# Inverses of the first two steps of a chunked recurrence: by doubling on TensorE instead of by elimination on VectorE

## The chip, the cores and the metric

One core of a Trainium2 chip. The metric is the device time of one execution in microseconds (us). Engines are named as in the profile: PE is TensorE (matmul), PEld its weight loads, DVE is VectorE, ACT is ScalarE, POOL is GpSimd, SP is SyncE, which here only issues DMAs. All data is fp32.

## What is computed

A recurrent attention block, and a feed-forward block on its output. For each of 4 batches and 8 heads, over 768 positions with head dimension 40:

```python
for t in range(S):
    y[:, :, t] = np.einsum('bhd,bhde->bhe', rt, state)
    Sa = np.einsum('bhde,bhe->bhd', state, at)
    state_decay = state * wt[:, :, None, :] - np.einsum('bhd,bhe->bhde', Sa, bt)
    state = state_decay + np.einsum('bhd,bhe->bhde', vt, kt)
```

Then, with the 8 x 40 head outputs of a token side by side as `x` (3072 tokens x 320):

```python
h = x @ w_in                          # 320 -> 1024
e = np.exp(h - h.max(-1, keepdims=True))
solu = h * e / (e.sum(-1, keepdims=True) + 1e-09)
ln = (solu - mean) / np.sqrt(var + 1e-06) * g_ln
out = ln @ w_out                      # 1024 -> 320
```

The weights arrive as 64-bit floats and are turned into fp32 on the chip from their bits.

## The kernel before, in words

The 768 positions are cut into 12 chunks of 64, the 4 batches into 2 pairs; that makes N = 24 steps, step `i` being chunk `i // 2` of pair `i % 2`. A step holds 16 units (2 batches x 8 heads), each with 64 x 64 matrices, so that a tile of 128 partitions x 512 holds all 16.

Within a chunk each position depends on the earlier ones through a strictly triangular 64 x 64 matrix per unit, `nt`; the kernel needs the inverse of (1 + `nt`), called `tu`. It comes about as follows:

- `decay` (ACT and PE: logarithm, running sum `pcum`, exponentials `ei` and `inv`), `decay_turned` (PE transposes `pei`, ACT copies to `ex`), `scaled` (POOL: keys `kb` from `raw_b` or `raw_k` and `inv`), `front` (PE transposes `pa`, `pb`; DVE makes `aT`, ACT `bT`), `norm` (PE products `pnt`; DVE masks them to `nt`, L340) prepare a step.
- `norm` also writes `nt` to DRAM (`nt_dram`). For each pair of steps (`GRP` = 2) `spread` reads it back so that each 32 x 32 diagonal block lies along a partition (`blk`), and `invert` eliminates column by column on DVE: 30 times a product (L392, `prod`) and a difference (L394, `uu`). It is a generator: `begin_inverse(n)` starts pair `n`, `some(k)` does `k` of its columns, so that the columns of a pair are strewn among other work by hand.
- The block inverses go to DRAM (`uu_dram`); `bring` loads them to `tu` and `uh`, `flip` (DVE, L419) transposes a block, and `couple` and `close` (PE `py`, `pz`; ACT `wy` and a copy) build the off-diagonal block, which completes `tu`.
- With it the main chain of a step runs: `attend_kv` and `attend_rs` (transposes `pk`, `pv`, `pr`, `pst`), `scores` (PE `ps`; DVE masks to `psi` and into `lv`), `carried` and `driven` (`px`), `solved` (`pu`), `answered` (`pl`; DVE masks to `lu`), `read` (`pyo`), `leave` (DVE, POOL: output `x` and new state).
- Later by 2 to 4 turns follow the feed-forward parts: `hidden` (`h`), `exped`, `weighed`, `spreadof`, `folded` (`plnT`), `output` (`po`).

Two more kinds of work stand beside these. `narrow(k)` does `k` of the 18 weight splits (64-bit to fp32, seven DVE and two ACT instructions each, L177 to L191); the weights are fetched by `land`. `centre_w2` (L210, L211) subtracts the mean from the second weight once, at i = 4, when all 18 splits are done.

The order on PE, POOL, DVE and SP is the order in which the Python code issues; only ACT's queue is left to a scheduler. A prologue prepares steps 0 to 4 and inverts pair 0; then the loop runs from i = -1. In turn `i` it does the main chain of step `i`, the preparation of step `i + 5` (`AHEAD`), and the feed-forward of earlier steps. Turn -1 has no main chain: it finishes `tu`, scores and weights ahead of step 0. The shares of columns and splits for the first turns are written by hand:

```python
shares = {-1: (0, 8, 6), 0: (0, 9, 7), 1: (0, 9, 6), 2: (0, 9, 6), 3: (0, 9, 6)}
narrowed = {-1: (0, 2), 0: (1, 2), 1: (1, 3), 2: (1, 2), 3: (1, 1)}
```

PSUM: `banks` are two tiles of two banks (`pnt`, `ps`, `px`, `pu`, `pl`, `pyo`, `py`, `pz`), `bank` two of one bank (transposes, `po`), and `h` is one tile of two banks, which the early `decay` also used for its running sum.

Of the kernel before, what the change touches and what calls it, by code (L numbers as in the profile page):

```python
# [16 lines left out]
P = 128  # L17
# [4 lines left out]
AHEAD = 5  # L22
LANDS_NEXT = {2: 6, 3: 7, 5: 8, 6: 9, 7: 10, 8: 11, 10: 12}
LAG = 1
LN_EXP = "natural_log_exp_and_others"


def shape_constants():
    s, t = np.arange(P)[:, None], np.arange(P)[None, :]
    same = s // C == t // C  # L30
    row = np.arange(P)[:, None] % C
    parts = dict(
        ident=np.eye(P),
        cum=same & (s <= t),
        tri=row < np.arange(C)[None, :],
        eye_hi=row == Q + np.arange(Q)[None, :],
        neg_hi=-(row >= Q).astype(np.float64),
        mean=np.full((P, P), 2.0 ** -10),
    )
    at, where = 0, {}  # L40
    for name, x in parts.items():
        where[name] = (at, at + x.shape[1])
        at += x.shape[1]
    return np.concatenate([np.asarray(x, np.float64) for x in parts.values()], 1).astype(np.float32), where


@with_exitstack
def kernel(
# [86 lines left out]
    def bank(name):  # L135
        return ps3.tile([P, 512], FP32, tag="bank", name=name)
# [78 lines left out]
    def half(p):  # L215
        return slice(C * p, C * p + C)
# [40 lines left out]
    def ok(i):  # L257
        return 0 <= i < N
# [29 lines left out]
    def decay(i):  # L288
        if not ok(i):
            return  # L290
        d = st[i]
        lw = two.tile([P, DM], FP32, tag="lw", name="lw", bufs=1)
        nc.scalar.activation(out=lw, in_=d["raw_w"].rearrange("p h d -> p (h d)"), func=AF.Ln)
        t = (bank("pcum") if i > 5 else ps2.tile([P, DFF], FP32, tag="h", name="h"))[:, 0:DM]
        nc.tensor.matmul(t, lhsT=c_("cum"), rhs=lw, start=True, stop=True)  # L295
        nc.scalar.activation(out=ei_t[0][:, :, 0:D], in_=heads(t), func=AF.Exp)
        inv = d["inv"] = two.tile([P, DM], FP32, tag="inv", name="inv", bufs=4)
        nc.scalar.activation(out=inv, in_=t, func=AF.Exp, scale=-1.0)

    def scaled(i, names="bk"):  # L300
        if not ok(i):
            return
        d = st[i]
        kb = d["kb"] = kb_t[i % (AHEAD + 2)]
        for n in names:
            j = H * (n == "b")
            nc.gpsimd.tensor_tensor(out=kb[:, j:j + H, 0:D], in0=d["raw_" + n], in1=heads(d["inv"]), op=ALU.mult)
# [31 lines left out]
    def masked(dst, t):  # L339
        nc.vector.tensor_tensor(out=dst, in0=t.rearrange("p b (j c) -> p b j c", j=4),  # L340
                                in1=tri.unsqueeze(1).unsqueeze(1).to_broadcast([P, 2, 4, C]), op=ALU.mult)
# [9 lines left out]
    def norm(i):  # L351
        if not ok(i):
            return
        d = st[i]
        t = banks("pnt")
        for u in in_turn(lambda p, q, g, h: (h, p ^ h)):
            p, q, g, h = u
            j = 2 * q + g
            mm(t[half(p ^ h), h, j * C:j * C + C], keyed(d["bT"], u), keyed(d["aT"], u))
        nt = d["nt"] = tokens("nt", AHEAD)  # L360
        masked(nt, t[:, :, 0:256])
        n, at = divmod(i, GRP)
# [5 lines left out]
    def spread(n):  # L370
        nb = two.tile([P, Q, Q], FP32, tag="blk", name="blk")
        for y in range(2):
            for e in range(2):
                home = C * y + Q * e
                queue = nc.gpsimd if y and not n else nc.sync
                queue.dma_start(out=nb[home:home + Q], in_=blocks[n][:, Q * e:Q * e + Q, Q * e:Q * e + Q])
        return nb

# [22 lines left out]


    def bring(i):
        if not ok(i):
            return
        d = st[i]
        d["tu"], d["uh"] = tu_t[i % 2], uh_t[i % 2]
        n, at = divmod(i, GRP)
        src = inverse[n].rearrange("(e a h x) c t -> e a h x c t", e=2, a=GRP, x=2)
        for x in range(2):  # L410
            nc.sync.dma_start(out=d["tu"][C * x:C * x + Q, :, Q:2 * Q], in_=src[0, at, :, x].rearrange("h c t -> c h t"))
        for x in range(2):
            nc.sync.dma_start(out=d["uh"][C * x + Q:C * x + C], in_=src[1, at].rearrange("h x c t -> c (h x) t"))

    def flip(i):
        if not ok(i):
            return
        tu = st[i]["tu"]
        nc.vector.transpose(out=tu[:, :, 0:Q], in_=tu[:, :, Q:2 * Q])  # L419

    def couple(i):
        if not ok(i):
            return
        d = st[i]
        t = banks("py")
        for u in in_turn(lambda p, q, g, h: (p ^ h, p)):
            p, q, g, h = u
            j = 2 * q + g
            x = half(p ^ h)
            mm(t[half(p), h, j * Q:j * Q + Q], d["nt"][x, h, j], d["tu"][x, 4 * h + j, 0:Q])  # L430
        nc.scalar.activation(out=wy[:, :, :, 0:Q], in_=t[:, :, 0:4 * Q].rearrange("p h (j c) -> p h j c", j=4),  # L431
                             func=AF.Copy, scale=c_("neg_hi"))

    def close(i):
        if not ok(i):
            return
# [267 lines left out]
    for i in range(2):  # L704
        load_keys(i, "w")
        load_keys(i, "b", nc.scalar)
        load_keys(i, "a")
    nc.scalar.dma_start(out=g_rows, in_=moe_g_ln.rearrange("(c p) -> c p", p=P))
    load_keys(2, "w")
    for n in range(3):  # L710
        land(n, nc.sync)
    decay(0)
    decay_turned(0)
    for i in range(4):
        scaled(i, "b")
        if i == 3:
            scaled(0, "k")
            scaled(1, "k")
        front(i)
        decay(i + 1)  # L720
        norm(i)
        decay_turned(i + 1)
        if i == 0:
            load_keys(2, "ba")
        if i == 1:
            load_keys(3, "w")
            begin_inverse(0)
            narrow(3)
            load_keys(3, "ba")
            load_keys(0, "k")  # L730
            load_keys(4, "w")
            some(8)
        if i == 2:
            load_values(0)
            load_keys(1, "k")
            some(8)
    load_keys(5, "w")
    load_keys(4, "ba")
    begin_inverse(1)
    for i in (2, 3):  # L740
        load_keys(i, "k", nc.gpsimd)
    by_value(0)
    scaled(2, "k")
    load_keys(4, "k", nc.gpsimd)
    scaled(3, "k")
    scaled(4)
    decay(5)
    load_keys(6, "w")
    land(3, nc.sync)
    some(14)  # L750
    narrow(1)
    bring(0)
    load_keys(5, "bak")
    load_values(1)
    for n in (4, len(lands)):
        land(n, nc.sync)
    load_keys(6, "bak")
    load_keys(7, "w")


    shares = {-1: (0, 8, 6), 0: (0, 9, 7), 1: (0, 9, 6), 2: (0, 9, 6), 3: (0, 9, 6)}
    narrowed = {-1: (0, 2), 0: (1, 2), 1: (1, 3), 2: (1, 2), 3: (1, 1)}
    for i in range(-1, N + 3 + LAG):
        j, m = i + AHEAD, i - LAG
        pieces = shares.get(i, (3, 6, 6))
        some_weights = narrowed.get(i, (0, 0))
# [84 lines left out]
```

## Time and profile before

| | |
|---|---|
| median of 3 runs | 663.46 us (662.98 to 663.58) |
| the profiled execution | 663.51 us |
| its span in the profile | 661.7 us |
| mean granted PE clock | 0.90 |
| PE busy | 572.6 us (87%) |
| DVE busy | 490.0 us (74%) |
| ACT busy | 238.9 us (36%) |
| POOL busy | 216.4 us (33%) |
| `uu` L394 and `prod` L392 on DVE, 360 each | 108.8 and 107.8 us |

Shares of busy time are means over a start in which the engines wait for each other and a long even stretch. The profile page also has the span in 40 slices of 16.5 us; the digits are tenths of busy time. A timeline row gives start and length in us, engine, line, operation, output and inputs, shapes, count, and in brackets the idle time of the engine before it with what ended it. A row of PE counts each fp32 product as two passes (`x32` for 16 products).

### The profile page before, as it was taken

The page shows a single profiled execution, that of the slowest core. Times are in us where ns is not written, and L with a number is a line of the kernel's source. Part 1 is how long each engine was busy: PE and PEld are TensorE (multiplying, and loading weights), DVE is VectorE, ACT ScalarE, POOL GpSimd, SP SyncE. Part 2 cuts the span into 40 slices and gives each one's busy share as a digit, 9 for nine tenths or more (in the row PEclk, how much of TensorE's full clock was granted, in tenths as well). Part 3 has the DMA queues.
Part 4 walks back from the last instruction along what each step waited for, and adds up shares of the span by engine and source line. Part 5 has one row for each costly group of instructions (what it writes and reads, how often), then busy time and mean ns, then how long its engine had stood idle before and what let it go on. Part 6 is the DMA issues. An engine that isn't in the chain of part 4 may idle for free.

```text
span 661.7 us, 26730 instructions
## 1 busy us (share of the span) xinstructions
PE 572.6 (87%) x11449; PEld 408.2 (62%) x11449; DVE 490.0 (74%) x1344; ACT 238.9 (36%) x494; POOL 216.4 (33%) x384
## 2 busy tenths in 40 slices
PE   5246674778698999999999999999999999999995
PEld 3134553665565767766776677667766767666653
DVE  4777977888995978888879788888797888423431
ACT  4213333333341443444344334433443233332221
POOL 2342304155050444144315431543244313422200
PEclk9565668659598999999999999999999999999998
DMA  8958976456343645455466465553442412310000
GB/s 165 159 101 132 169 136 106 108 106 124 62 87 62 114 84 108 90 112 107 87 109 114 85 114 89 108 108 77 75 86 58 96 39 48 70 36 26 23 20 20
DMA packets 276749, 59.93 MB, mean 91 GB/s; under 512 B 264656, under 2 KB 274488, under 8 KB 276632
## 3 DMA queue, kind: packets, MB, share of 16 engines
q1 hardware_dynamic: 263384, 44.96, 38.9%
q0 software_dynamic: 7856, 8.76, 5.5%
q10 hardware_dynamic: 5392, 4.51, 2.4%
q8 instruction: 90, 1.47, 0.9%
q14 instruction: 27, 0.22, 0.1%
HBM read 40.10 MB, written 13.37 MB: 81 GB/s over the span
## 4 chain that ended last, share of the span: by engine, by line
PE 73%; DVE 12%; DMA 6%; issue 3%; ACT 2%; SPq 2%; POOL 0%; DVEq 0%; ACTq 0%; POOLq 0%
PE h L232 16%; PE po L680 15%; PE pyo L232 8%; PE ps L232 4%; PE px L232 4%; PE plnT L669 3%; PE pu L232 3%; DVE uu L394 3%; DVE prod L392 3%; PE pk L312 2%; PE pz L232 2%; PE pl L232 2%; PE pcum L295 2%; PE pv L312 2%; PE pnt L232 2%
## 5 line engine op out<-in xcount | busy, mean ns | idle before, releaser
L232 PE MATMUL h<-w_in,xT 128*128 128x512 f32 (+1 forms) x288 | 120.9, 612 | 0.0
L394 DVE TENSOR_TENSOR uu<-uu,prod 128x30 f32<-128x30 f32 (+4 forms) x360 | 108.8, 302 | 12.4
L680 PE MATMUL po<-w,lnT 128*128 128x320 f32 x384 | 115.0, 445 | 3.0 <-DVE w L211 3.0
L392 DVE TENSOR_TENSOR prod<-blk,uu 128x30 f32<-128x30 f32 (+4 forms) x360 | 107.8, 299 | 11.7 <-DMA blk<-nt_dram 1.5
L680 PEld LDWEIGHTS po<-w,lnT 128*128 128x128 f32 x384 | 71.0, 191 | 33.0 <-issue 6.5
L658 POOL TENSOR_TENSOR rs<-c,mhalf 128x1 f32<-128x1 f32 x24 | 13.4, 558 | 194.3 <-DVE c L657 194.3
L600 POOL TENSOR_TENSOR st<-tot,ex 104x160 f32<-104x160 f32 x44 | 21.2, 499 | 135.1 <-DVE tot L596 125.2
L632 DVE TENSOR_REDUCE nmax<-h 128x1 f32<-128x1024 f32 x24 | 29.3, 1221 | 35.6 <-PE h L232 35.6
L232 PEld LDWEIGHTS h<-w_in,xT 128*128 128x128 f32 (+1 forms) x288 | 38.7, 189 | 21.5 <-issue 19.3
L612 POOL DMA_DIRECT2D xT<-x x96 | 48.6, 511 | 0.0
L670 ACT COPY lnT<-plnT 128x512 f32<-128x512 f32 x48 | 26.2, 588 | 43.9 <-PE plnT L669 43.9
L232 PE MATMUL pyo<-lv,kb 64*64 64x104 f32 x768 | 39.1, 277 | 2.7
L232 PE MATMUL pyo<-lu,kb 64*64 64x104 f32 x768 | 37.8, 270 | 0.0
L635 ACT ACTIVATE e<-h,nmax 128x1024 f32<-128x1024 f32 x24 | 26.7, 1113 | 30.5 <-DVE nmax L632 29.4
L431 ACT ACTIVATE wy<-py,cst 128x256 f32<-128x256 f32 x24 | 11.4, 473 | 69.0 <-PE py L232 69.0
L581 DVE TENSOR_TENSOR x<-pyo,ex 104x256 f32<-104x256 f32 x48 | 18.1, 419 | 24.2 <-PE pyo L232 23.2
L254 POOL DMA_DIRECT2D raw_r<-in_r_dram x48 | 34.8, 726 | 1.1 <-issue 1.1
L641 DVE TENSOR_TENSOR e<-h,e 128x1024 f32<-128x1024 f32 x24 | 29.4, 1224 | 7.5 <-ACT e L635 7.2
L649 DVE BATCH_NORM_STATS2 bs<-e 128x6 f32<-128x512 f32 x48 | 30.9, 685 | 0.8
L514 ACT COPY x<-px 128x320 f32<-128x320 f32 x24 | 10.2, 426 | 56.4 <-PE px L232 56.4
L232 PEld LDWEIGHTS ps<-aT,kT 40*64 40x64 f32 x768 | 15.5, 153 | 23.9 <-DVE lu L340 14.3
L684 ACT ACTIVATE osb<-po,rs 128x320 f32<-128x320 f32 x24 | 12.7, 527 | 48.5 <-PE po L680 35.3
(124 smaller groups left out, 1135.5 us busy)
## 6 DMA issues: line engine op xcount, KB each, us to landing
nt_dram<-nt SPq DMA_DIRECT2D x24, 256.0 KB
blk<-nt_dram SPq DMA_DIRECT2D x46, 128.0 KB
raw_w<-in_w_dram SPq DMA_DIRECT2D x48, 80.0 KB
a<-in_a_dram SPq DMA_DIRECT2D x48, 80.0 KB
raw_r<-in_r_dram POOLq DMA_DIRECT2D x48, 80.0 KB, 3.4
lv<-in_v_dram SPq DMA_DIRECT2D x48, 80.0 KB
out_dram<-osb ACTq DMA_DIRECT2D x24, 160.0 KB
raw_b<-in_b_dram SPq DMA_DIRECT2D x44, 80.0 KB
```

Source lines behind the costliest of these rows:

```text
L232: nc.tensor.matmul(o, lhsT=lhsT, rhs=rhs, start=start, stop=stop, skip_group_check=True)
L254: queue.dma_start(out=x[half(p), :, 0:D], in_=ap[2 * bp + p, :, ci * C:(ci + 1) * C, :].rearrange("h t d -> t h d"))
L312: nc.tensor.transpose(out=t[0:W2, j * P:(j + 1) * P], in_=x[:, 2 * j:2 * j + 2].rearrange("p a b -> p (a b)")[:, 0:W2], identity=ident)
L392: nc.vector.tensor_tensor(out=t, in0=nb[:, j:j + 1, j + 1:Q].to_broadcast([P, n_c, m]), in1=u[:, 0:n_c, j:j + 1].to_broadcast([P, n_c, m]) ...
L394: nc.vector.tensor_tensor(out=u[:, 0:n_c, j + 1:Q], in0=u[:, 0:n_c, j + 1:Q], in1=t, op=ALU.subtract)
L612: nc.gpsimd.dma_start(out=xT[to:to + Q, 2], in_=x[at + P - 3 * D:at + D, 2])
L632: nc.vector.tensor_reduce(out=nmax, in_=d["h"], axis=AX.X, op=ALU.max, negate=True)
L635: nc.scalar.activation(out=e, in_=d["h"], func=AF.Exp, bias=nmax, accum_out=d["esum"])
L641: nc.vector.tensor_tensor(out=d["e"], in0=d["h"], in1=d["e"], op=ALU.mult)
L649: nc.vector.bn_stats(out=bs[:, x], in_=d["e"][:, x * 512:x * 512 + 512])
L670: nc.scalar.copy(out=lnT[:, x * (NF // 2):(x + 1) * (NF // 2)].rearrange("p f t -> p (f t)"), in_=t)
L680: nc.tensor.matmul(d["out"][:, 0:DM], lhsT=d["lnT"][:, f, :], rhs=w2[:, f, :], start=f == 0, stop=f == NF - 1)
```

## The change

For steps 0 and 1 (`DOUBLED` = 2) `tu` is no longer made by elimination, DRAM and coupling. `norm` leaves `ntm` = `nt` less the identity in SBUF instead of sending `nt` to DRAM, and a new generator `double` builds the inverse of (1 + `nt`) by doubling the size of the inverted diagonal blocks six times, from 1 to 64. It carries the inverse `x` and its transpose `xt`. One doubling is three rounds of 16 products of 64 x 64: `pw` (with `ntm` and `xt`), a DVE multiplication by a mask of signs (`w_`), then `pxt` and `pxx`, which ACT and DVE copy back to SBUF as `xt` and `x`; in the last one there is no `pxt`, and `pxx` is copied into `tu` (step 0's by ACT, step 1's by DVE). The masks are a new constant, `levels`, loaded on ACT's queue.

The prologue is written anew: the two chains (`chains`) advance in turn, and between their twelve half-doublings stand the preparation of steps 2, 3 and 4, the start of pair 1 (`begin_inverse(1)`, three times `some(2)`), and keys, values and scores of step 0. After them come `some(8)`, `narrow(3)`, loads and the landing of weights. Turn -1 is gone. In turns 0 to 3 the splits are 4, 4, 4 and 3 where they were 3, 4, 3 and 2; the others have moved from before turn 0, where 6 stood and 3 are left. `bring`, `flip`, `couple` and `close` do nothing for steps 0 and 1. `decay` always uses `bank` for its running sum. Pair 1's `blk` is loaded half by POOL, as pair 0's was.

```diff
+DOUBLINGS = 6
+DOUBLED = 2
...
-        t = (bank("pcum") if i > 5 else ps2.tile([P, DFF], FP32, tag="h", name="h"))[:, 0:DM]
+        t = bank("pcum")[:, 0:DM]
...
         masked(nt, t[:, :, 0:256])
+        if i < DOUBLED:
+            d["ntm"] = tokens("psi", 2)
+            nc.vector.tensor_tensor(out=d["ntm"], in0=nt, in1=level(0).to_broadcast([P, 2, 4, C]), op=ALU.subtract)
+            return
...
+    def double(i):
...
+        for k in range(DOUBLINGS):
+            y = lambda u: away(u, k)
+            t, w_at = products(banks("pw"), lambda u: d["ntm"][half(on(u)), u[3], 2 * u[1] + u[2]],
+                               lambda u: xt_[xt_at[u]] if k else one(on(u)), on, y)
+            nc.vector.tensor_tensor(out=w_, in0=t, in1=level(k + 1).to_broadcast([P, 2, 4, C]), op=ALU.mult)
+            yield
+            x = lambda u: x_[x_at[u]] if k else one(y(u))
+            last = k == DOUBLINGS - 1
+            if not last:
+                t, xt_next = products(banks("pxt"), x, lambda u: w_[w_at[u]], y, on)
+                nc.scalar.copy(out=xt_, in_=t)
+            t, x_next = products(ps2.tile([P, DFF], FP32, tag="h", name="pxx").rearrange("p (b c) -> p b c", b=2),
+                                 lambda u: w_[w_at[u]], x, y, on if last else lambda u: away(u, k + 1))
+            if last:
+                for at in range(2):
+                    for b in range(2):
+                        copy = nc.vector.tensor_copy if i % 2 else nc.scalar.copy
+                        copy(out=tu[half(at), (at ^ b)::2, Q:], in_=t[half(at), b])
+            elif i % 2:
+                nc.scalar.copy(out=x_, in_=t)
+            else:
+                nc.vector.tensor_copy(out=x_, in_=t)
...
+            yield
...
-                queue = nc.gpsimd if y and not n else nc.sync
+                queue = nc.gpsimd if y and n == 1 else nc.sync
...
     def bring(i):
-        if not ok(i):
+        if not ok(i) or i < DOUBLED:
             return
...
+    def front_(i):
+        scaled(i, "b")
+        front(i)
+
+    def norm_2():
+        decay(3)
+        norm(2)
+        decay_turned(3)
+
+    def norm_3():
+        norm(3)
+        scaled(0, "k")
+        begin_inverse(1)
+        load_keys(2, "k")
+        decay(4)
+
+    def keys_0():
+        by_value(0)
+        attend_kv(0)
+        scaled(1, "k")
+        load_keys(5, "ba")
+
+    def norm_4():
+        norm(4)
+        decay(5)
+        some(2)
+
+    def keys_1():
+        attend_rs(0)
+        some(2)
+        load_keys(3, "k")
+        load_keys(6, "w")
+
+    def scores_0():
+        decay_turned(5)
+        scores(0)
+        some(2)
+
+    chains = [double(i) for i in range(DOUBLED)]
+    for between in (None, lambda: front_(2), norm_2, lambda: front_(3), norm_3, lambda: decay_turned(4), None,
+                    lambda: front_(4), keys_0, norm_4, keys_1, scores_0):
+        for x in chains:
+            next(x)
+        if between:
+            between()
...
+    some(8)
+    narrow(3)
...
-    shares = {-1: (0, 8, 6), 0: (0, 9, 7), 1: (0, 9, 6), 2: (0, 9, 6), 3: (0, 9, 6)}
-    narrowed = {-1: (0, 2), 0: (1, 2), 1: (1, 3), 2: (1, 2), 3: (1, 1)}
-    for i in range(-1, N + 3 + LAG):
+    shares = {0: (4, 8, 4)}
+    narrowed = {0: (1, 3), 1: (1, 3), 2: (1, 3), 3: (1, 2)}
+    for i in range(0, N + 3 + LAG):
```

More of the change, by code (lines that the diff above doesn't have):

```diff
@@ L44, in shape_constants, with doubling_constants @@
     return np.concatenate([np.asarray(x, np.float64) for x in parts.values()], 1).astype(np.float32), where
+def doubling_constants():
+    r, c = np.arange(P)[:, None] % C, np.arange(C)[None, :]
+    parts = [r == c]
+    for k in range(DOUBLINGS):
+        m = 2 ** k
+        parts.append(-((r == c) | ((r // m % 2 == 1) & (c // m == r // m - 1))).astype(np.float64))
+    return np.concatenate([np.asarray(x, np.float64) for x in parts], 1).astype(np.float32)
 @with_exitstack
@@ L97, in c_ @@
         return cst[:, lo:hi]
+    levels = const.tile([P, (DOUBLINGS + 1) * C], FP32, name="levels")
     ident, tri = c_("ident"), c_("tri")
@@ L366, in norm, with level, products @@
                           in_=nt.rearrange("p h j c -> p (h j) c"))
+    def level(k):
+        return levels[:, k * C:(k + 1) * C].unsqueeze(1).unsqueeze(1)
+    def products(t, lhsT, rhs, src, dst):
+        count, place = {}, {}
+        for h in range(2):
+            for q in range(2):
+                for g in range(2):
+                    for p in range(2):
+                        u = (p, q, g, h)
+                        at = (src(u), dst(u))
+                        place[u] = (half(at[1]), at[0], count.get(at, 0))
+                        count[at] = count.get(at, 0) + 1
+        t = t[:, :, 0:256].rearrange("p b (j c) -> p b j c", j=4)
+        for u in in_turn(lambda *u: (src(u), dst(u))):
+            mm(t[place[u]], lhsT(u), rhs(u))
+        return t, place
@@ new lines, in double @@
+    def double(i):
+        d = st[i]
+        tu = d["tu"] = tu_t[i % 2]
+        both = two.tile([P, DFF], FP32, tag=("e", "lnT")[i], name="both", bufs=1)
+        both = both.rearrange("p (w b j c) -> p w b j c", w=2, b=2, j=4)
+        x_, xt_ = both[:, 0], both[:, 1]
+        w_ = two.tile([P, 4, P], FP32, tag="s", name="w_").rearrange("p (b j) (two c) -> p b (j two) c", b=2, two=2)
+        on = lambda u: u[0] ^ u[3]
+        away = lambda u, k: on(u) ^ u[2] ^ (u[1] if k % 2 == 0 else 0)
+        one = lambda where: levels[half(where), 0:C]
+        x_at = xt_at = None
+        for k in range(DOUBLINGS):
+            y = lambda u: away(u, k)
[19 more added lines that the diff above has]
+                nc.vector.tensor_copy(out=x_, in_=t)
+            if not last:
+                x_at, xt_at = x_next, xt_next
+            yield
@@ L415, in flip @@
     def flip(i):
-        if not ok(i):
+        if not ok(i) or i < DOUBLED:
             return
@@ L421, in couple @@
     def couple(i):
-        if not ok(i):
+        if not ok(i) or i < DOUBLED:
             return
@@ L434, in close @@
     def close(i):
-        if not ok(i):
+        if not ok(i) or i < DOUBLED:
             return
@@ L707 @@
         load_keys(i, "a")
+    nc.scalar.dma_start(out=levels, in_=nc.inline_tensor(doubling_constants(), name="levels").ap())
     nc.scalar.dma_start(out=g_rows, in_=moe_g_ln.rearrange("(c p) -> c p", p=P))
     load_keys(2, "w")
-    for n in range(3):
-        land(n, nc.sync)
+    load_keys(2, "a")
     decay(0)
     decay_turned(0)
-    for i in range(4):
+    for i in range(2):
         scaled(i, "b")
-        if i == 3:
-            scaled(0, "k")
-            scaled(1, "k")
+        if i == 0:
+            load_keys(2, "b", nc.gpsimd)
+            load_keys(0, "k", nc.gpsimd)
         front(i)
@@ L722 @@
         decay_turned(i + 1)
[L723 to L736, printed above, removed]
-    load_keys(5, "w")
[L738 to L741, printed above, removed]
@@ L742 @@
-    by_value(0)
+    load_keys(3, "wba")
+    load_values(0)
+    load_keys(4, "wba")
+    load_keys(1, "k")
+    load_keys(5, "w")
+    for n in (0, 1):
+        land(n, nc.sync)
+    def front_(i):
[16 more added lines that the diff above has]
+        load_keys(5, "ba")
@@ L743 @@
+    load_values(1)
     scaled(2, "k")
-    load_keys(4, "k", nc.gpsimd)
+    load_keys(4, "k")
     scaled(3, "k")
[L746 to L754, printed above, removed]
+    load_keys(5, "k")
+    scaled(4, "k")
+    scaled(5)
+    load_keys(6, "bak")
+    decay(6)
+    for n in (2, 3):
+        land(n, nc.sync)
+    load_keys(7, "wbak")
+    load_keys(8, "w")
+    some(8)
+    narrow(3)
@@ L755 @@
     for n in (4, len(lands)):
         land(n, nc.sync)
-    load_keys(6, "bak")
-    load_keys(7, "w")
-    shares = {-1: (0, 8, 6), 0: (0, 9, 7), 1: (0, 9, 6), 2: (0, 9, 6), 3: (0, 9, 6)}
-    narrowed = {-1: (0, 2), 0: (1, 2), 1: (1, 3), 2: (1, 2), 3: (1, 1)}
-    for i in range(-1, N + 3 + LAG):
+    shares = {0: (4, 8, 4)}
+    narrowed = {0: (1, 3), 1: (1, 3), 2: (1, 3), 3: (1, 2)}
+    for i in range(0, N + 3 + LAG):
         j, m = i + AHEAD, i - LAG
@@ L768 @@
         some(pieces[0])
-        if i >= 0:
-            bring(i + 1)
-            load_values(i + 2)
+        bring(i + 1)
+        load_values(i + 2)
         carried(i)
@@ L777 @@
         load_keys(j + 4, "w")
-        if i >= 0:
-            by_value(i + 1)
+        by_value(i + 1)
         some(pieces[1])
@@ L787 @@
         hidden(m - 2, ((2, 0), (2, 1)))
-        if i >= 0:
-            flip(i + 1)
+        flip(i + 1)
         exped(m - 2)
@@ L807 @@
         scores(i + 1)
-        if i < 0:
-            flip(i + 1)
         couple(i + 1)
```

## The prediction

> **What bounds the kernel now.** I read the 40 slices first, to see where TensorE (PE) isn't full:
>
> ```profile
> PE   5246674778698999999999999999999999999995
> DVE  4777977888995978888879788888797888423431
> PEclk9565668659598999999999999999999999999998
> ```
>
> A slice is 16.5 us. From slice 13 on PE is full and its clock whole; before that, up to about 200 us, PE is half idle at half clock and VectorE (DVE) is the busy one. Only there can this change act. Next the table by stretch, cut where `px` starts a step (PE, weight loads, DVE, ACT, POOL busy, clock, DMA):
>
> ```profile
> 17.00:27.00 10.00, 1.55 (x7) 1.15 (x8) 6.89 (x24) 3.15 (x8) 3.20 (x4) 0.57 0.90 173
> 27.00:45.00 18.00, 8.47 (x87) 5.94 (x85) 13.36 (x42) 4.24 (x9) 5.69 (x9) 0.59 0.52 88
> 45.00:58.00 13.00, 3.58 (x11) 2.23 (x12) 11.34 (x34) 2.32 (x6) 7.47 (x11) 0.50 1.12 191
> 70.30:96.60 26.30, 17.94 (x387) 15.05 (x387) 21.70 (x63) 9.65 (x26) 5.48 (x9) 0.63 0.86 150
> 122.20:153.50 31.30, 23.00 (x462) 18.32 (x457) 26.59 (x77) 11.69 (x24) 11.02 (x19) 0.59 0.49 102
> 237.80:260.00 22.20, 21.95 (x487) 15.67 (x486) 17.48 (x49) 9.23 (x19) 9.15 (x16) 1.00 0.62 113
> ```
>
> A settled step takes 22.2 us and is PE's (21.95 busy). Steps 0 to 3 take 25.6 to 31.3 us and are DVE's: pairs of inverses and weight splits fill it. Step 4 (184 to 215) is PE's again, but for 3.0 us in which `po` waits for DVE's L211. What arrives earlier at the end of step 4 ends the kernel earlier, one for one. Third, the waits of PE up to 160 us:
>
> ```profile
> PE pnt L232 <- DVE aT L336: 8.6, 2, 5.9
> PE pk L312 <- DVE aT L336: 7.7, 2, 4.2
> PE ps L232 <- DVE lu L340: 7.0, 3, 5.4
> ```
>
> PE waits for small DVE products that stand in the queue behind inverse steps and splits. Last, DVE in order of time:
>
> ```profile
> 27.91 0.42 DVE L386 TENSOR_SCALAR uu<-blk 64x512 f32<-64x512 f32 x1 [3.24 <-DMA blk<-nt_dram]
> 54.09 0.19 DVE L394 TENSOR_TENSOR uu<-uu,prod 128x15 f32<-128x15 f32 x1
> 66.56 0.68 DVE L340 TENSOR_TENSOR lv<-ps,cst 128x512 f32<-128x512 f32 x1
> 88.47 0.65 DVE L340 TENSOR_TENSOR lu<-pl,cst 128x512 f32<-128x512 f32 x1
> 104.58 0.98 DVE L386 TENSOR_SCALAR uu<-blk 64x512 f32<-64x512 f32 x1 [1.65 <-DMA blk<-nt_dram]
> ```
>
> Pair 0 (steps 0 and 1) holds DVE from 27.9 to 54.3, after a round trip through DRAM; step 0's last score mask, `lv`, ends at 67.2. I call that moment T; it divides what the change replaces from what it reshuffles.
>
> [...]
>
> ```profile
> 15.61 0.69 PE L232 MATMUL pnt<-aT,bT 40*64 40x64 f32 x32 [0.19 <-ACT bT L321]
> 22.50 1.07 PE L312 MATMUL pa<-cst,a 128*104 128x128 f32 x4 [5.61 <-DMA a<-in_a_dram]
> 34.53 1.13 PE L232 MATMUL pnt<-aT,bT 40*64 40x64 f32 x32 [5.85 <-DVE aT L336]
> ```
>
> The same 16 products (32 passes) take 0.69 us warm and 1.13 after a long idle. [...] Here a 128x512 eviction costs 0.69 us on DVE (`nt`) and 0.59 on ACT (`ex`), as much as the block of products that fills it.
>
> **The change part by part.**
>
> *Removed for steps 0 and 1.* DVE: pair 0's 64 operations, 19.9 us busy, plus two transposes (0.9). Also the DRAM round trip, the `tu`/`uh` loads, and `couple`/`close` of both steps (32 products, 4 blocks on PE, 4 ACT copies).
>
> *Added on DVE.* Two `ntm` subtractions, 12 products `w_`, 5 copies: 19 x 0.69 = 13.1 us; 4 copies of 64x256 at about 0.35 (the `tu` copies of 128x256 take ACT 0.35) = 1.4. So 14.5 against 20.8: DVE has 6 us less to do.
>
> *Added on PE.* 12 blocks `pw`, 10 `pxt`, 12 `pxx` of 16 products 64x64. The nearest row is `pu` (64x64), warm: a block issues in 0.52 us (73.12 to 73.63). 34 x 0.52 = 17.7 us warm, 34 x 0.9 = 31 cold. ACT gets 15 copies x 0.59 and four small ones: 10 us, in queue order between `ex` and `bT`.
>
> *T, worked as a chain.* `pnt` of step 1 and `pei` of step 2 end at 16.9 and PE is warm; nothing ahead of that changes length, since the fetched weights that no longer stand first only ease the DMA. One doubling of both chains, warm: `pw` A and B 1.04; 0.43 wait for `w_` A (its block ends 0.69 after its start, DVE takes 0.69, the hand-over about 0.1: 1.47 less the 1.04 that B covers); `pxt` A, `pxx` A, `pxt` B 1.56; 0.42 until DVE has emptied the one `pxx` buffer; `pxx` B 0.52. That is 3.97. Six, less the absent last `pxt`, plus 1 for the copies between the last two `pxx`: 23.8. Between them stand three fronts (1.0 each), three `norm` (0.52), three `pcum` (0.73), three `pei` (0.5), `pk pv pr` (1.4) and scores (1.1): 10.8 warm, of which about 1.8 fills the waits. 16.9 + 23.8 + 9.0 = 49.7. To this I add what stands in a queue ahead: `kb` of step 4 on POOL behind the two `blk` loads, which wait for `nt_dram` of step 3 (2.8 us to land at 20.39; about 1.5); pair 1's four set-up operations and two steps on DVE ahead of the last `w_` (2.0); DVE's four copies and the two masks after the scores (2.5). T = 55.7; 1.8 for small waits that I don't see: 57.5, so T is 9.7 earlier than 67.2. The lowest I can argue is 54.
>
> *The loop, handed back.* Slot -1 had splits and steps in it; they move. From T to `lu` of step 0 before: 21.3 us. After: 44 pair operations x 0.33, 4 splits x 2.3 (three took 6.9 from 17 to 23.9) and `aT` 0.6 = 24.3, so +3.0. From `lu` 0 to `lu` 1 before 25.6; after: one split more (+2.3), six small pair operations fewer (-1.4), and the wait on `blk` goes (-2.8): there SP sent `nt_dram` only at 95.4, 5.7 us after `nt` was ready, behind loads; after, those loads are issued in the prologue. -1.9. `lu` 2 to `lu` 3: one more 320-wide split, +2.8. Step 3's tail: one more, +2.8, less the 1.0 that DVE waits for `pmean`: +1.8. Sum +5.7.
>
> *No cost:* moved loads on SP and POOL (SP issues 28 loads at 0.65 by about 19 us, the last needed near 32; POOL's four for `raw_b` 2 and `raw_k` 0 take 2.8 between two `kb` that are 3.3 apart); `levels`, 229 KB on ACT's queue, is needed at 13.7; `pcum` in the small bank costs 0.2 of waiting for `aT`. If that cover fails, PE waits in the chain one for one, and the last two cases hold it.
>
> *Sum:* -9.7 + 5.7 = -4.0 us on the profiled execution's 663.51 (span 661.70, 1.8 around it), which is the median 663.46 within 0.05. **659.5 us.** Break-even is T = 61.5.
>
> **What no row shows.** Whether PE stays warm through gaps of 0.4 us every 2 us: from 153.4 to 165.8 it does, with one of 1.5; from 171 to 184 it stays cold for 13 us with gaps of 0.6. Bounds: no loss, or all cold: PE work 31 + 20 = 51, and the waits vanish behind it, T = 72. I take warm. The wait on `blk` going: 0 to -4.4. Pair operations beside POOL take 0.2 to 0.9 each: +-2 on the loop. Below nothing: DVE's outliers may fall by 2 with POOL quieter.
>
> **The rivals.** (a) *Clock lost*: [...] Against: PE hardly rests in this order. T = 72 gives 663.5 + 10.5 = 674; half of it, 668. Decides from T = 61.5 on. Slower. (b) *Queue stall*: pair 1's `blk` is late and holds `w_` on DVE, or `nt_dram` holds POOL's `kb`. `nt_dram` took 5.8 at 95.4, not 2.8: +3 to +6 there, 663 to 666. (c) *All handed back*: the wait on `blk` stays (+2.8) and two of the four splits take 2.9, as the one from 54.2 to 57.1 did beside other ACT work (+1.2): 663.5. (d) *The doubling finishes at 54 and DVE gains from quiet*: 653. That the change doesn't act is excluded by the instruction order: pair 0 is gone.
>
> **How the numbers follow.** Forecast 0.50, (a) 0.20, (b) 0.10, (c) 0.12, (d) 0.08. 0.2% (1.3 us) is about what a measurement of this kernel can tell from no change. The forecast is faster but for 0.05; (d) faster; (c) half same, half slower; (a) and (b) slower but for 0.02. Faster 0.53, same 0.13, slower 0.34. Range 652 to 674: (d) to (a); the forecast's own is 655 to 663.
>
> **What would show it.** `lv` of step 0 near 57; clock above 0.9 from 17 to 55; `pnt` near 0.69; `w_` waiting for `pw` under 0.5 us each; `lu` of step 0 near 82; no wait on `blk` in step 1; `px` of step 4 near 178. Wrong if T is over 61.5, or if T is early and `px` 4 isn't.

## The result, and the profile after

| | before | after |
|---|---|---|
| median | 663.47 us (662.98 to 663.58) | 674.40 us (671.9 to 675.65) |
| ratio after / before | | 1.0162, 95% interval 1.0130 to 1.0194 |
| profiled execution, its span | 663.51, 661.7 us | 675.65, 673.8 us |

The change makes the kernel 1.6% slower; the forecast was 659.5, and 674.40 lies 0.4 above the range.

The slices of the page after, to be held against those of before (a slice is now 16.8 us):

```profile
PE   4777454667687999999999999999999999999995
DVE  4437887788597787878888879788888888433431
PEclk9999556658679999999999999999999999999998
```

In the second to fourth slice PE's clock is now 9 tenths or more (5, 6, 5 before) and PE 7 tenths busy, as intended (2, 4, 6 before). In the same slices VectorE has fallen to 4, 3, 7 from 7, 7, 7. Behind them PE's clock is again 5 or 6 tenths for five slices and everything looks as it did, only longer. The table by stretch of the kernel after shows the two stages (PE, weight loads, DVE, ACT, POOL busy, clock, DMA):

```profile
17.00:27.00 10.00, 7.78 (x299) 6.30 (x302) 5.00 (x7) 4.18 (x9) 0.87 (x1) 1.00 0.78 124
27.00:37.00 10.00, 7.71 (x234) 6.28 (x229) 2.78 (x5) 4.05 (x8) 1.70 (x2) 0.83 0.48 122
37.00:47.00 10.00, 7.70 (x358) 6.38 (x350) 4.27 (x7) 3.56 (x8) 4.49 (x7) 1.00 0.49 98
47.00:57.00 10.00, 8.45 (x318) 7.01 (x314) 4.23 (x8) 5.39 (x11) 1.77 (x3) 1.00 0.29 56
67.00:77.00 10.00, 5.47 (x78) 4.24 (x79) 9.41 (x22) 3.29 (x7) 5.97 (x9) 0.53 0.84 179
```

From 17 to 57 PE is 7.7 to 8.5 of 10 busy and VectorE 2.8 to 5.0. Ten microseconds behind T it is the other way round. VectorE in order of time, after, at the points that the prediction named:

```profile
64.36 0.68 DVE L353 TENSOR_TENSOR lv<-ps,cst 128x512 f32<-128x512 f32 x1
91.97 0.68 DVE L353 TENSOR_TENSOR lu<-pl,cst 128x512 f32<-128x512 f32 x1
120.94 0.65 DVE L353 TENSOR_TENSOR lu<-pl,cst 128x512 f32<-128x512 f32 x1
182.76 0.67 DVE L353 TENSOR_TENSOR lu<-pl,cst 128x512 f32<-128x512 f32 x1
```

| us | before | predicted | after |
|---|---|---|---|
| T (end of `lv` 0) | 67.2 | 57.5 | 65.0 |
| T to `lu` 0 | 21.3 | 24.3 | 27.0 |
| `lu` 0 to `lu` 1 | 25.6 | 23.7 | 29.0 |
| `lu` 1 to `lu` 2 | 28.3 | 28.3 | 26.2 |
| `lu` 2 to `lu` 3 | 28.0 | 30.8 | 35.6 |
| `px` of step 4 | 184.8 | 178 | 196.9 |

The 178 is the forecast's own sign; its sum doesn't give it, 184.8 less 4.0 is 180.8. In these two executions `px` of step 4 is 12.1 us later and so is the end (the medians lie 10.9 apart; the profiled execution after is the slowest of its four). T gained 2.2 instead of 9.7, and the turns 0 to 3 lost 14.3 instead of 5.7.

**VectorE's account.** The view that shows where the time went is VectorE's own busy time up to `px` of step 4, cut near T (length, busy, then clock and DMA). Before:

```profile
0.00:65.00 65.00, 44.29 (x143) 0.67 0.78 140
65.00:184.79 119.79, 99.37 (x294) 0.68 0.60 114
```

After:

```profile
0.00:65.00 65.00, 30.77 (x69) 0.97 0.62 117
65.00:196.90 131.90, 104.31 (x318) 0.62 0.52 104
```

VectorE was busy for 143.7 us up to there and now for 135.1, 8.6 less. But its idle time (length less busy) went from 20.7 to 34.2 in the first 65 us, and from 20.4 to 27.6 in the rest: 41.1 in all before, 61.8 after. 20.7 more idle less 8.6 less busy is the 12.1 lost. That sum comes out by definition; it says where the time is, not why. Nor are the 8.6 all saved: after the change PE gets to `px` of step 4 while VectorE still has the last operations of turn 3 ahead of it. Cut where VectorE ends one and the same operation, `tot` of step 3, before and after:

```profile
0.00:183.97 183.97, 142.91 (x435) 0.68 0.67 123
0.00:199.26 199.26, 137.17 (x392) 0.74 0.55 107
```

That is 43 operations and 5.7 us less to do, close to the predicted 6, and 21.0 us more idle. VectorE itself is 15.3 us later there; step 4 gives 3 of them back (see step 3's tail). The reading to be tested: the work that VectorE didn't do beside the doublings (four more splits behind T, pair 1's columns) has to be done behind them, where VectorE is what everything waits for. e5 tests it.

**Gaps of PE.** T wasn't 57.5 either. PE in order of time, after:

```profile
18.80 0.69 PE L245 MATMUL pw<-levels,psi 64*64 64x64 f32 x32
...
22.50 0.28 PE L245 MATMUL pxx<-levels,w__322 64*64 64x64 f32 x3 [0.70 <-issue]
...
26.78 0.46 PE L245 MATMUL pw<-both,psi 64*64 64x64 f32 x15 [0.54 <-issue]
...
32.80 0.51 PE L245 MATMUL pxt<-w__342,both 64*64 64x64 f32 x20 [2.29 <-issue]
...
33.91 1.09 PE L325 MATMUL pa<-cst,a 128*104 128x128 f32 x4
...
41.82 0.27 PE L245 MATMUL pxt<-w__342,both 64*64 64x64 f32 x1 [1.01 <-issue]
```

Eight gaps stand in the stage, 0.46 to 2.29 us, 6.8 in all, released by "issue", so by nothing that the profile shows, and mostly in the middle of a block whose operands are all there. Between one and the next lie 127 or 128 recorded passes, once 255. A pass is a weight load and a matmul; 128 passes are 256 instructions. The page of the kernel after has, in its list of DMA queues (packets, MB, share):

```profile
q8 instruction: 98, 1.61, 1.0%
```

The page counts 12,409 matmuls and as many weight loads, which is 253 of PE's instructions to one of these 98 packets (before: 11,449 of each and 90 packets, 254). So I read these gaps as PE waiting for its next instructions. That is an inference from the counts, and no view shows it: near the longest gap, which runs from 30.51 to 32.80, packets of this queue begin between 30 and 31 and between 33 and 34.

### The profile page after: what moved, and what is told of

Read it like the earlier page. It is cut to its first block, busy times and chain, and to the rows that moved or that the text cites. A ratio compares the mean times of both kernels' runs of the same rounds, so it can differ in the third digit from the quotient of the medians.

```text
span 673.8 us, 28636 instructions
## 1 busy us (share of the span) xinstructions
PE 585.6 (87%) x12409; PEld 417.4 (62%) x12409; DVE 481.7 (71%) x1301; ACT 246.4 (37%) x509; POOL 215.4 (32%) x382
## 4 chain that ended last, share of the span: by engine, by line
PE 64%; DVE 3%; issue 2%; DMA 1%; ACT 0%; DVEq 0%; ACTq 0%
PE h L245 15%; PE po L757 15%; PE pyo L245 6%; PE px L245 4%; PE plnT L746 3%; PE ps L245 3%; PE pu L245 3%; PE pl L245 2%; PE pz L245 2%; PE pk L325 2%; PE pcum L308 1%; PE py L245 1%; PE pa L325 1%; PE pr L325 1%; PE pst L540 1%
## 5 line engine op out<-in xcount | busy, mean ns | idle before, releaser
L245 PE MATMUL h<-w_in,xT 128*128 128x512 f32 (+1 forms) x288 | 122.7, 622 | 0.0
L757 PE MATMUL po<-w,lnT 128*128 128x320 f32 x384 | 113.6, 441 | 3.6 <-DVE w L224 3.6
L471 DVE TENSOR_TENSOR uu<-uu,prod 128x30 f32<-128x30 f32 (+4 forms) x330 | 98.9, 300 | 11.4
L469 DVE TENSOR_TENSOR prod<-blk,uu 128x30 f32<-128x30 f32 (+4 forms) x330 | 98.3, 298 | 9.1
L757 PEld LDWEIGHTS po<-w,lnT 128*128 128x128 f32 x384 | 70.4, 190 | 33.2 <-issue 6.4
L747 ACT COPY lnT<-plnT 128x512 f32<-128x512 f32 x48 | 26.1, 588 | 41.1 <-PE plnT L746 41.1
L712 ACT ACTIVATE e<-h,nmax 128x1024 f32<-128x1024 f32 x24 | 26.7, 1113 | 32.0 <-DVE nmax L709 31.0
L245 PE MATMUL pyo<-lu,kb 64*64 64x104 f32 x768 | 37.8, 270 | 0.0
L658 DVE TENSOR_TENSOR x<-pyo,ex 104x256 f32<-104x256 f32 x48 | 18.1, 420 | 24.3 <-PE pyo L245 23.3
L308 PE MATMUL pcum<-lw,cst 128*128 128x320 f32 x48 | 21.9, 541 | 13.7 <-ACT lw L306 13.4
L325 PE MATMUL pv<-cst,v 128*104 128x128 f32 x96 | 16.4, 299 | 19.9 <-POOL v L298 17.9
L508 ACT ACTIVATE wy<-py,cst 128x256 f32<-128x256 f32 x22 | 10.4, 473 | 62.9 <-PE py L245 62.9
L349 DVE TENSOR_TENSOR aT<-pa,ex 104x512 f32<-104x512 f32 x24 | 16.5, 687 | 21.9 <-PE pa L325 14.4
```

The source lines that it names most:

```text
L245: nc.tensor.matmul(o, lhsT=lhsT, rhs=rhs, start=start, stop=stop, skip_group_check=True)
L325: nc.tensor.transpose(out=t[0:W2, j * P:(j + 1) * P], in_=x[:, 2 * j:2 * j + 2].rearrange("p a b -> p (a b)")[:, 0:W2], identity=ident)
L469: nc.vector.tensor_tensor(out=t, in0=nb[:, j:j + 1, j + 1:Q].to_broadcast([P, n_c, m]), in1=u[:, 0:n_c, j:j + 1].to_broadcast([P, n_c, m]) ...
L471: nc.vector.tensor_tensor(out=u[:, 0:n_c, j + 1:Q], in0=u[:, 0:n_c, j + 1:Q], in1=t, op=ALU.subtract)
L712: nc.scalar.activation(out=e, in_=d["h"], func=AF.Exp, bias=nmax, accum_out=d["esum"])
L757: nc.tensor.matmul(d["out"][:, 0:DM], lhsT=d["lnT"][:, f, :], rhs=w2[:, f, :], start=f == 0, stop=f == NF - 1)
```

## The experiments

Twelve kernels. Each ratio is against the kernel before, run beside it. T, `lu` and `px` are from one profiled execution each, which can be its kernel's fastest (e3, e7, e9) or slowest (the kernel after, e11). The kernel after, e3, e4 and e8 have the same code up to T: in their four executions T is 63.0 to 65.0, and PE's longest gap near 32 us is 1.19 to 2.56. So a difference of 2 us in T alone shows nothing. Except where said, the edit is to the kernel after.

### e1: the constants on another queue

In the kernel after, the first `lw` on ACT starts at 7.71 instead of 6.14:

```profile
5.49 0.62 ACTq L785 DMA_DIRECT2D levels<-levels  x1
6.94 0.72 ACTq L786 DMA_DIRECT2D g_rows<-in_moe_g_ln_dram  x1
7.71 0.47 ACT L306 ACTIVATE lw<-raw_w 128x320 f32<-128x320 f32 x1 [5.68 <-DMA raw_b<-in_b_dram]
```

```diff
-    nc.scalar.dma_start(out=levels, ...)
+    nc.gpsimd.dma_start(out=levels, ...)
```

> The changed kernel, with the constant levels loaded on POOL's queue instead of ACT's. Theory (ACT's issue of levels holds the first logarithm back): lw of step 0 starts at 6.1 us again instead of 7.7, T comes 1.6 earlier and the whole ends near 672.8. Rival (the first keys come late whatever the queue, since levels adds 229 KB to a full DMA): lw stays at 7.7, no change from 674.4.

Measured: 1.0168 (1.0145 to 1.0191). `lw` is back at 6.17. In all seven kernels with `levels` on ACT's queue it starts at 7.22 to 7.71, in the seven others at 6.14 to 6.35, so that DMA did cost the start 0.9 to 1.6 us. T, 63.1, lies within what the same code shows without this edit. Nothing reached the end that the intervals could tell.

### e2: the loads of step 1 ahead of SP's wait

SP in the kernel after stands still from 48.2 to 56.3, at `nt_dram` of step 4, with the keys and values of the next steps behind it:

```profile
46.85 1.32 SPq L267 DMA_DIRECT2D a<-in_a_dram  x2
56.29 0.39 SPq L382 DMA_DIRECT2D nt_dram<-nt  x1
56.77 1.29 SPq L267 DMA_DIRECT2D raw_k<-in_k_dram  x2
```

```diff
     def keys_0():
         by_value(0)
         attend_kv(0)
         scaled(1, "k")
+        load_keys(3, "k")
+        load_values(1)
+        load_keys(6, "w")
         load_keys(5, "ba")
```

with the three later places taken out.

> The changed kernel, with raw_k of step 3, raw_w of step 6 and the values of step 1 loaded before norm of step 4, so that on SP they no longer stand behind nt_dram of step 4. Theory (SP is blocked from 48.2 to 56.3 and POOL's keys then crowd between 66 and 74, beside the pair operations on DVE): POOL is done earlier, pb of step 5 no longer waits 2.4 us, pair operations after T fall from 0.8 to 0.3 us, lu of step 0 about 3 earlier: 671. Rival (DVE's time there is its own work): lu of step 0 stays within 1 us of 92, 674.

Measured: 1.0143 (1.0125 to 1.0162), 0.2% less than the kernel after, with intervals that overlap. T to `lu` 0 fell from 27.0 to 24.8, close to the predicted 24.3 (e1, e4, e7 and e8 stay at 26.6 to 27.0). This wait was real; at the end it is worth too little to be told by itself.

### e3: the splits earlier

```diff
-    narrow(3)
+    narrow(6)
...
-    narrowed = {0: (1, 3), 1: (1, 3), 2: (1, 3), 3: (1, 2)}
+    narrowed = {0: (1, 2), 1: (1, 3), 2: (1, 2), 3: (1, 1)}
```

> The changed kernel, with the loop's splits as before the change (3, 4, 3, 2) and the three others in the prologue (6 instead of 3). The work is the same. Theory A (a third split after the scores delays tot, then POOL's state and v, then pv, then pcum, then on ACT the scale of the next split): lu of step 0 is 7 later, but the waits of DVE on ACT scale in turn 3 (6.7) go and each tail is a split shorter: 671, and the sum of DVE's waits on ACT scale under 7 instead of 12.7. Rival B (DVE's work is what counts, wherever it stands): 674, no change.

Measured: 1.0158 (1.0143 to 1.0173). `lu` 0 moved to 96.4, 4.4 later; `lu` 2 to `lu` 3 fell from 35.6 to 28.6; the total is where it was. The wait for ACT in turn 3 went, but the same 18 splits had still to be done behind T.

### e4: the scale on VectorE

VectorE's waits for ACT, kernel after, 66 to 200 us (total, times, longest):

```profile
DVE bits L201 <- ACT scale L192: 12.7, 3, 6.7
```

```diff
-        act(out=scale, in_=scale, func=AF.Copy, scale=2.0 ** 23, bias=-(1023 - 127) * 2.0 ** 23)
+        ts(out=scale, in0=scale, scalar1=-(1023.0 - 127.0), scalar2=2.0 ** 23, op0=ALU.add, op1=ALU.mult)
```

> The changed kernel, with the exponent's scaling of each split on DVE instead of ACT: 18 DVE instructions of about 0.3 us more (5.3 us). Theory A (DVE stands still because ACT has this scale in its queue behind ei of a late pcum): the 12.7 us of waits go, lu of steps 1 and 3 then wait for pl at most: 669 to 672. Rival B (DVE's work is what counts): slower by the added work, 679.

Measured: 1.0207 (1.0186 to 1.0228), slower than the kernel after. The same view for e4:

```profile
DVE w L203 <- ACT w L199: 6.2, 2, 5.8
DVE w_in L203 <- ACT w_in L196: 5.0, 2, 4.8
```

The wait went to the split's second ACT instruction, 11.2 us where 13.5 had been, and VectorE got an operation more for each split. What is late is ACT's queue, not the scale.

### e5: four splits inside the doublings

A split becomes a generator that yields behind each VectorE operation, and the loop over the twelve half-doublings takes four operations behind each of the fifth to the eleventh, 28 in all, which are four splits:

```diff
         for x in chains:
             next(x)
+        halves += 1
+        if 5 <= halves < 12:
+            bits_(4)
...
-    narrow(3)
+    narrow(2)
```

with e3's `narrowed`.

> Four weight splits (28 VectorE operations, 2.4 us each split) are issued inside the doublings, four operations behind each mask or copy of doublings 2 to 5; two follow the doublings instead of six, and the loop's splits are those of e3 (3, 4, 3, 2). Theory A (the loss is VectorE's idle time: in the first 65 us VectorE is busy 30.8 us after the change against 44.3 before, so it stands 34 us idle there against 21, and everything up to step 4 is VectorE's to do): VectorE's busy time in 20 to 65 rises by about 9.6 from 21.4, T moves by less than 1.5, lu of step 0 goes from e3's 96.4 to about 87, and the time from e3's 673.1 to about 664. Theory B (VectorE's gaps in the doublings are too short, so that the splits delay the w_ masks and with them PE's chain one for one): T moves later by 6 to 9.6 and the time stays at 671 to 674. Theory C (what ACT does late bounds the loop, not VectorE): lu 0 is early, but the time is given back as waits on ACT: about 670.

Measured: 1.0058 (1.0030 to 1.0086), against 1.0158 for e3: the splits' move is worth 1.0%, 6.6 us of the 9.6 that were moved. VectorE's account of e5:

```profile
0.00:65.00 65.00, 39.90 (x95) 0.95 0.63 119
65.00:187.56 122.56, 101.83 (x299) 0.65 0.56 111
```

9.1 more busy in the first 65 us than after the change; idle there 25.1 instead of 34.2, and 45.8 up to `px` 4 instead of 61.8. e3 and e5 differ in nothing but the place of four splits, so this is the experiment that shows the cause: VectorE's idle time beside the doublings. T is 65.7, 0.7 above the 63.0 to 65.0 of the unchanged code: if the chain of the doublings pays, it's little, far from theory B's 6 to 9.6. `lu` 0 came at 90.1, not at 87.

### e6: e1, e2 and e5 together

> The same splits in the doublings, with the constants on GpSimd's queue (as e1) and the loads of e2. Theory A: e1's start (about 1.5 us at lw, 0 to 1.5 at the end) and e2's 1.2 us come on top of e5: about 661 to 663, between 0.4% faster and as fast as the kernel before. Theory B: 669 to 672. Theory C: 668.

Measured: 0.9977 (0.9960 to 0.9994): now faster than before. `px` of step 4 is at 181.7, VectorE's idle time up to it 40.5. The edits of e1 and e2, alone worth nothing or 0.2%, bring 0.8% on top of e5; which of the two does, no run tells. VectorE in order of time in e6, inside the doublings:

```profile
38.83 0.69 DVE L463 COPY both<-pxx 128x512 f32<-128x512 f32 x1 [0.84 <-PE pxx L268]
39.44 0.41 DVE L205 SCALAR_TENSOR_TENSOR w<-w,scale 128x256 int32<-128x256 int32 x1
39.77 0.42 DVE L208 SCALAR_TENSOR_TENSOR w_in<-w,w_in 128x256 f32<-128x256 int32 x1
40.22 0.42 DVE L210 TENSOR_TENSOR w_in<-w_in,w 128x256 f32<-128x256 f32 x1
40.56 0.29 DVE L190 TENSOR_SCALAR scale<-w 128x256 int32<-128x256 int32 x1
41.70 0.69 DVE L446 TENSOR_TENSOR w__322<-pw,levels 128x512 f32<-128x512 f32 x1 [0.85 <-PE pw L268]
```

Four operations of a split lie between a copy and a mask, and VectorE still waits 0.85 us for the block of products: they cost the chain nothing there.

### e7: the first weights behind the doublings

```diff
-    for n in (0, 1):
-        land(n, nc.sync)
...
-    for n in (2, 3):
+    for n in (0, 1, 2, 3):
```

> The kernel after the change with the first two weight loads (1 MB, which land from 24 to about 31 us) issued behind the doublings instead of ahead of them. Theory F (PE's gaps every 128 products are fetches of its instructions, and the fetch due near 31 us stands behind this 1 MB on the DMA engines): the gap of 2.29 us at 32.8 falls to 0.5 to 0.7 like the others, the blocks behind it run at full clock, and T comes 2.5 to 4 us earlier (from 65.0 to 61 to 62.5), while the gaps remain as many as before. Theory G (the gap there is a wait of another kind, which the profile doesn't name): the gap stays at about 2.3 and T within 0.7 us. The time: the weights land later, so the first splits may wait; 669 to 676 under either.

Measured: 1.0166 (1.0142 to 1.0191). PE in order of time in e7, the same place in the same block:

```profile
31.71 0.51 PE L245 MATMUL pxt<-w__336,both 64*64 64x64 f32 x20 [0.28 <-issue]
...
32.67 0.65 PE L325 MATMUL pa<-cst,a 128*104 128x128 f32 x4
```

The gap of 2.29 is 0.28, where the same code with the weights ahead of it shows 1.19 to 2.56; `pa` takes 0.65 instead of 1.09, and nine gaps are still there, none over 0.74. So the gap is as theory F asked: it's long where the 1 MB of weights is on its way. T is 62.6, just outside the 63.0 to 65.0, and not as early as the theory's 61 to 62.5 either. That the gaps are fetches at all is inferred, from the counts of passes and of packets, and from this. The time didn't move: as in e1, what helped the stage ahead of T brought the end nothing that could be told.

### e8: the decay behind the turn's splits

```diff
         spreadof(m - 2)
-        decay(j + 2)
...
         narrow(some_weights[1])
+        decay(j + 2)
         some(pieces[2])
```

> The kernel after the change with the decay of step i+7 (ln, cumulative sum, two exponentials) issued behind the splits at the end of a turn, so that on ACT the splits' scale and mantissa no longer stand behind ei, which waits for pcum and so for v. If the 12.7 us of VectorE's waits on ACT's scale are what the loop lost: they fall to under 3 us, lu 3 goes from 182.8 to about 173 and the time to 664 to 667. If VectorE then waits for the next late thing (ps, px or the state), the waits move there: time within 2 us of 673.

Measured: 1.0139 (1.0113 to 1.0166), 0.2% under the kernel after, with intervals that overlap. VectorE's waits for ACT in e8:

```profile
DVE bits L201 <- ACT scale L192: 5.1, 4, 2.1
DVE w L201 <- ACT scale L192: 2.1, 2, 1.4
```

13.5 became 7.2, about half of what the first theory asked, and `lu` 3 came at 174.6 instead of 182.8, nearly as it asked. The end didn't follow: from `lu` 3 to `lu` 5 this execution took 57.1 us, the kernel after 54.6. 1.5 of that is the first `po` of turn 4, 3.86 us where the kernel after has 2.39; by its length that is PE's clock, and chance (see step 3's tail below). One later step took 24.2 instead of 22.2: there VectorE waited 1.71 us for a load of `blk`, and one `prod` took 2.55 us; with `aT` behind them, PE stood still for 1.76 ahead of `pv`. Why the load was late stays open.

### e9 to e11: e6 with more of the same

e9 is e6 with the edit of e8; e10 is e6 with `land(1)` issued in `norm_2`, behind step 2's `norm`, instead of ahead of the doublings; e11 is both.

> e6 with the decay behind the turn's last splits (as e8). VectorE still waited 5.3 us for ACT's scale in e6's loop. If that wait was VectorE's loss: up to 3 us faster than e6, 659 to 661 against 663.5 of the kernel before. If VectorE's other waits (9.0 us for ps) take it over: within 1 us of e6.

> e6 with the second weight load (0.5 MB) issued behind step 2's norm instead of ahead of the doublings. Theory F (the fetch of instructions due near 32 us stands behind the weights): the gap of 1.74 us at 32.4 falls to about 1 or less, T 1 us earlier; the time 661 to 662, 1 us better than e6 at the most. If the second load delays the loads of step 5 or the next fetch: no gain or 1 to 2 us worse.

> e9 and e10 together. e9 and e10 each measured 0.9926 of the kernel before (intervals 0.9898 to 0.9953, 0.9905 to 0.9947), e6 0.9977. If the two gains are independent: 0.987 to 0.990. If both only fill the same idle time of VectorE: 0.992.

Measured: e9 0.9926 (0.9898 to 0.9953), e10 0.9926 (0.9905 to 0.9947), e11 0.9923 (0.9903 to 0.9943). VectorE's account of e9:

```profile
0.00:65.00 65.00, 42.31 (x104) 0.97 0.71 130
65.00:178.56 113.56, 98.44 (x290) 0.68 0.57 114
```

Idle 22.7 and 15.1, 37.8 in all where the kernel before had 41.1; `px` of step 4 at 178.6. But this is the fastest of e9's six executions, 656.88 against a median of 660.50. In e10 the gap of 1.74 at 32.4 is gone (there is one of 1.18 at 35.7 and one of 0.82 at 26.7). T is 62.9 instead of e6's 64.8 in both; e9 has the same code as e6 up to T, so T alone shows no gain of an edit here. The gains don't add: e11 is no better than either. e10 gained more than the 1 us that I had allowed, and its profile (span 658.4, e6's 658.9) doesn't show by what; the order of these three kernels and their distance to e6 are not settled, that they beat both kernels is.

### e12: the edit of e8 on the kernel before

> The kernel before with one edit: the decay behind the turn's last splits, as in e8 and e9. It asks whether e9's gain over the kernel before needs the doubling. Before the change VectorE waits for ACT's scale for 2.2 us in all from 66 to 230. If the edit only takes such waits away: 0 to 2 us faster, 0.997 to 1.000. If it helps PE and the state by itself: 0.993, and then the doubling would be worth nothing beside it.

Measured: 1.0025 (1.0010 to 1.0040). Neither reading: without the doublings the edit loses a quarter of a percent. So e9's 0.7% isn't to be had by that edit alone. Whether some other rearrangement by hand would speed up the kernel before as much, no run tries.

## Why the prediction was wrong, point by point

- **T, 57.5 predicted, 65.0 measured (7.5 off; 5.5 to 7.5 in the four executions of the same code).** The chain's sum of 23.8 priced blocks and hand-overs rightly: where nothing interferes, two blocks of `pw` issue in 1.2 us and `pxt` and `pxx` follow at 0.5, as `pu` had promised. It had no term for the gaps of PE, by the inference above its instruction supply: 6.8 us of them (4.4 to 6.8 in the four) and, behind the longest, 1.3 of half clock (0.50 granted from 33.55 to 36.96; `pa`, `pb`, `pw` 3.9 us from start to start after, 2.6 in e7, where the clock was 1.00). And "nothing ahead of that changes length" failed: `pw` A started at 18.8, not 16.9, of which e1 gives 1.5 to `levels` on ACT's queue. Together 10.0, against the 7.5 that were missing, so that other terms must have been set too high; which, isn't worked out here.
- **"`levels` on ACT's queue: no cost."** Wrong by 1.5 us at the start, worth little at the end (e1).
- **The loop, +5.7 predicted, +14.3 measured.** The step that failed is the method: I moved operations between stages, each at its price, kept the waits between them as they were, and took T's gain as a gain of the end, though my own first part had said that VectorE bounds everything up to step 4. A T of 57.5 with 14.5 us of new work on VectorE in place of 20.8 means VectorE idle beside the doublings; I never summed that idle time. The forecast's own numbers imply 43.4 us of it up to `px` 4 (41.1 before, plus 6.3 of work less, less 4.0 for the earlier end); it was 61.8, and 13.5 of the 20.7 more lie in the first 65 us. e5 filled 9.1 of these and won 6.6; e1 and e7, which act on the stage ahead of T, won nothing that could be told.
- **Its parts.** T to `lu` 0: +5.7 for +3.0, and e2 shows most of the rest (2.2) as SP's wait. `lu` 0 to `lu` 1: +3.4 for -1.9; the wait on `blk` did go, but one on ACT of 5.1 us took its place. `lu` 1 to `lu` 2: -2.1 for 0; 1.0 of it is that two of the four splits there now have 256 columns (2.3 us) in place of 320 (2.8), the rest stays unexplained. `lu` 2 to `lu` 3: +7.6 for +2.8, with 6.7 of such a wait. In turn 3 it is a chain across four engines (the kernel after, in order of time):

```profile
167.48 1.09 PE L325 MATMUL pv<-cst,v 128*104 128x128 f32 x4 [4.21 <-POOL v L298]
...
177.41 0.81 PE L308 MATMUL pcum<-lw,cst 128*128 128x320 f32 x2
...
178.25 0.44 ACT L309 ACTIVATE ei<-pcum 128x320 f32<-128x320 f32 x1 [1.64 <-PE pcum L308]
...
179.76 0.49 DVE L201 SCALAR_TENSOR_TENSOR bits<-bits,scale 128x320 int32<-128x320 int32 x1 [6.71 <-ACT scale L192]
```

  `pv` waits for POOL's `v`, `pcum` comes 10 us later, ACT's `ei` waits for it, and the split's `scale` stands behind `ei` in ACT's order. Before, VectorE's waits of that kind came to 2.2 us in all. e3 and e8 cut them and moved the time little, e4 only moved them: they are part of the loss up to `lu` 3, and no lever by themselves in these runs.
- **Step 3's tail, +1.8.** `px` 4 doesn't show it: from `lu` 3 to there the kernel after is 0.3 shorter, since PE doesn't wait for that split. `lu` 4 does: 25.9 us behind `lu` 3, not 23.2, +2.7 for the split's predicted +2.8. From `lu` 4 to `lu` 5 it is lost again, 28.7 for 31.5. VectorE's wait of 1.0 for `pmean` goes, as predicted. Another 1.5 was luck. It is the first `po` of turn 4, before and after:

  ```profile
  201.94 3.84 PE L680 MATMUL po<-w,lnT 128*128 128x320 f32 x8 [3.01 <-DVE w L211]
  216.07 2.39 PE L757 MATMUL po<-w,lnT 128*128 128x320 f32 x8 [3.62 <-DVE w L224]
  ```

  After the longer wait the granted clock was 1.00 over these 2.39 us in this execution; in the kernel before it was 0.60 over the 3.84. That the span behind `px` 4 is 476.9 us in both profiles is so by this chance; in e1, with 4.61 us for the same `po`, it is 480.2.
- **Rival (a), clock lost, 674.** The number came true by chance, the mechanism didn't: the clock was 1.00 from 17 to 27 and 37 to 57, and the half clock (0.50) from 33.55 to 36.96 cost 1.3. T was 65.0, not 72. **(b)** was partly so: a queue did stall on `nt_dram`, SP's with the loads rather than POOL's with `kb`: 2.2 us at `lu` 0, little at the end (e2). **(c)** had the right kind, splits that take longer beside ACT work, at a tenth of the size. **(d)** asked for T at 54; no run came near it.
- **What held:** VectorE has 5.7 us less to do, 6 predicted; PE's clock stays at 1.00 through gaps of 0.4 to 1.0 us in the kernel after (from 36.96 to 67.6); the copies keep pace with the blocks, PE's waits for those of `pxx` coming to 0.7 us and, at the last, 1.4; the DRAM round trip of pair 0 is gone; `blk` no longer holds step 1.

## What to carry to other kernels

When work is moved off the engine that bounds a stage, sum that engine's busy and idle time up to the point where it stops being the bound, before and after, and cut both at the same operation: here 5.7 us less work came with 21.0 us more idle time, and the difference was the loss. In these runs the dependent chain on another engine paid only when the bounding engine had other work to put into its gaps. Splits of 2.4 us, issued four operations of 0.3 to 0.4 us at a time, turned +1.6% into +0.6%; with the edits of e1 and e2 it was -0.2%, with one more reordering -0.7%. Whether whole splits inside the chain would have done as well, no run tries.

## What the runs showed of the hardware

- In the doublings of the kernel after PE pauses every 127 or 128 recorded passes (once 255), for 0.46 to 1.01 us but for one pause. That one, near 31 us, with 1 MB of weights on its way, took 1.19 to 2.56 us in four executions of the same code, and 0.28 with the weights later (e7).
- PE's granted clock was 0.50 from 33.55 to 36.96 in the kernel after, behind a gap of 2.29 us. It also fell to 0.50, for about 3 us, behind single gaps of 2.56 (e8), 2.33 (e5, at 46.7) and 1.39 (e5, ahead of the last `pxx`), and in e9 behind gaps of 0.44 and 1.09 close together. Behind 2.01 (e5, at 32.4), 1.74 (e6) and the same 1.39 in the kernel after it stayed at 1.00. The first `po` of turn 4, behind waits of one length, in e1 and in e7:

  ```profile
  211.40 4.61 PE L757 MATMUL po<-w,lnT 128*128 128x320 f32 x8 [3.63 <-DVE w L224]
  211.88 2.39 PE L757 MATMUL po<-w,lnT 128*128 128x320 f32 x8 [3.63 <-DVE w L224]
  ```

  2.39 is what these products took at a granted clock of 1.00 in the kernel after, and 3.84 what they took at 0.60 in the kernel before. So in these runs the length of a gap alone doesn't decide: gaps of 1.39 to 2.56 us cost clock, and of two of 3.63 one, by the length of its `po`, did and one didn't. At this one place two executions differ by 2.2 us.
- With `levels` issued on ACT's queue at the start ACT's first `lw` came 0.9 to 1.6 us later (at 7.22 to 7.71 with it, 6.14 to 6.35 without; 7.71 in the kernel after, 6.17 in e1).
- From `lu` 5 to `lu` 17 a step takes 22.2 us in the kernels before and after alike, so a loss that is still there at `lu` 5 isn't made up by them.
